# Front and passage of a transformer block with a spatial gMLP: a new order, and new engines for 44 operations

## The chip, the cores and the metric

The kernel runs on one core of a Trainium2 chip, in bf16 with f32 accumulation. The core has five engines with an instruction stream each, which wait for one another only through semaphores: PE (TensorE, matmuls), ACT (ScalarE), DVE (VectorE), POOL (GpSimd) and SP (SyncE, which here only issues DMAs). The metric is the device time of one execution, in microseconds.

## What is computed

With D = 448, S = 2048, 16 heads of 28, a window of 256 keys and F/2 = 896:

```python
mod = (silu(c) @ w_mod)                       # six rows of 448: sa, ca, ga, sb, cb, gb
h = layernorm(x) * (1 + ca) + sa
q, k, v = heads(h @ wqkv)
p = softmax(window(q @ k.T * 28 ** -0.5))     # key i seen by query t if 0 <= t - i < 256
x = x + ga * ((p @ v) @ wo)
h = layernorm(x) * (1 + cb) + sb
z = gelu(h @ w_in)
z1, z2 = z[:, :896], layernorm(z[:, 896:])
g = w_sp @ z2 + b_sp[:, None]                 # w_sp is 2048 x 2048, over the rows
out = x + gb * ((z1 * g) @ w_out)
```

## The kernel before

The 2048 rows are 16 tiles of 128, in four blocks (tb 0 to 3) of four tiles. Everything stays in the core's buffer (x_sb, hT, KT, Vaug and so on). The work falls into three stages, with overlaps.

The front and the attention. The modulation row is made by small matmuls (L546 and L536) of silu(c) with w_mod. wo_g is wo times ga (L601, four multiplies of 112 x 448, one for each quarter of the rows of wo); WQK is the q and k weight laid out in 32 columns a head (L617 on DVE and POOL, L618 on ACT). QBD, a buffer for a narrow piece of q, is cleared by two L523 on ACT. For each block: statistics of x (L629, L631 on DVE, the power on POOL in L633), the normalised tile xn (L644 to L657), a transpose to hT (matmuls at L740 for block 0, DMA at L465 for the rest), scale and shift (L732, L749, L751), the projections (K in L821, q in L763 and L797, v in L841), each copied out of the accumulator banks ps by ACT or DVE (L833/L834, L772, L802, L815/L816, L790/L791, L845/L846). For each tile: scores (L956 in blocks of 32 rows, L967 for the narrow piece), exponential on ACT (L912, into PW or PT), mask on DVE (L973, L993), times V (L1000), division by the row sum (L1014, L1016, into o_sb), DMA transpose (L465), the output projection (L1026) and the sum with x (L1030).

The passage. As the last tiles of the attention run, the second norm of each finished tile is made (again L629 to L657, into one of three xn slots), transposed by DMA into hT (L465), scaled and shifted when a block's four tiles are there (L1051 on DVE or POOL, L1049 on ACT; four pieces per block), and multiplied with w_in: L1120 for z2 and L1141 for z1, with gelu on ACT (L1127, L1149). DVE takes the statistics of z2 (L629) and normalises it (L1132). Meanwhile SP issues the transposing loads of w_sp into wspA and wspB (16 each, L465; L461 is the helper, `turn`). They write into buffers that the scores, the masks and QBD used, so each waits for the last reader. SP's loads and transposes are issued in one order on one queue.

The gated part. L1166 multiplies w_sp with all 16 tiles of z2, so its first sum needs the last z2 tile. Then come b_sp (L1170), z1 (L1173), w_out (L1185) and the store.

What sets the order: the program first adds 1148 operations, each with the engines that may do it (`either` and `free` offer ACT or DVE, or also POOL), its dependencies and the buffer slots it takes. The string PLAN (lines 13 to 73) then gives for each its engine (p, a, d, t for POOL, s for SP), its number and, behind dots, its slot. `Sched.order` reads the words, `count` and `waits` work out the semaphore waits, and `emit` issues each engine's operations in the order in which they stand:

```python
        for at, word in enumerate(PLAN.split()):
            n, *slots = map(int, word[1:].split("."))
            ...
            op.eng = names[word[0]]
            ...
            self.prog[op.eng].append(op)
```

Nothing is reordered later: an engine whose next instruction waits holds back all behind it.

Of the kernel before, what the change touches and what calls it, by code (L numbers as in the profile page):

```python
# [13 lines left out]
s10 t36 p40.1 a7 s8 p69.2 a9 p75.3 d114 s12 p65.1 p53.0 t33 d112 p68.2 s11 t34 p54.3 d115 p77.0 d113 p50.3 s13  # L14
a41 p71.0 t116 a43 p46.0 s15 d117.0 t29 p74.2 d118.3 p62.0 p64.2 p47 a42 a44 p57.0 p48.1 d106 d86 p76.0 p49
a107 t104 p129.6 p67.3 d87 d105 p126.4 t37 a130 p82.3 p56.3 t111 p84.1 d127 p81.1 p73.1 a131 p83.3 p66.0 d128
t38 p72.0 p141.1 d110 d121 p78.0 a108 t109 p70.2 p150.3 d119 p142 d122 d120 p79.2 d184 p151 t123 a143 p138.0
a152 t28 d125.2 p139 d124.3 p85.0 p147.6 d178 a140 p132.2 d185 p148 d182 a133 p144.7 d179 d180 p135.1 a134
p153.0 d183 a136 d181 p371.0 d246 t186 a137 p145 d248 p154 a372.4 t39 p165.1 d187.3 t190 d242 s194 p166 t188
a149 t192 d45 p377.0 a146 d373 p156.6 d167 a378.6 t189.1 p157 d244 p159.7 t191.2 a158 p395.0 d193.0 a155 s196  # L20
d379 p172.6 a396.5 d249 d247 p173 d243 p175.1 a174 s197 p160 d88 t89 d245 a397 p176 d168 p94.0 t250 p95 d177
s195 a171 p402.0 a161 d96 t254 p97.1 t256 a403.1 p98 d398 s14 d375 p162.7 d400 p374.0 p163 a404 d381 p90.0 d99
p376 d201 a199 p422.0 d198 d251.0 p380 p382 d200 p91 s258 a423.0.0 p211.1 d93 d92 d407 p218.0 d170 d252 p212
d255.1 t253.2 a164 d383 s260 p429.0 d169 a213 t257.3 p219 a430.3 p399.1 p205.1 s16 d220 p206 d384.2 p202.0
d306 s385 p203 a207 d426 p401 p447.0 a204 p208.1 s804 a448.4.1 d310 p209 d405 p227.0 d431 p228 s259 t102
p424.1 p406 p408 a425 p454.0 d229 a210 d409 p427.0 d312 a455.1 p230.0 t101 d410.1 p221.1 p231 d451 s411 t103
p428 p222 a232 p80.3 p472.0 d456 s261 a223 p432 a215 p224.0 d216 a473.5.2 p225 d214 s21 p233.1 p433 s807
p449.0 d434 t100 d226 a217 p479.0 d435.0 a450 t262 p234 d308 s436 a480.0 p474.0 p236.0 t263 d311 d313 d235
p452.0 p237 d476 s806 p453 a475 p496.0 a238 d307 d481 t265 d264 p412.1 a497.3.0 p457 p386.0 p387 p458 d309
d459 d388 d460.1 t314 t320 p413 p498.0 p521.0 a499 a522.1.1 p272.0 d414 p523.0 p273 p269.1 p477.0 s461 p270  # L30
d415 d274 d321.2 d316 s20 p503.0 a271 d500 t317.3 p275.0 p478 s323 p276 p266.1 p482 p267 a504.4 a524 p546.0
p483 t318 d389 d277 d319.1 a268 d505 d484 p282.0 d390 d278 p283 a547.5.2 p437.1 p548.0 p438 s18 d485.1 d525
p501.0 p528.0 d439 d440 d315.0 s486 s325 a284 a529.0 a549 a279 p502 p288.0 p291.1 p289 p292 d290 p553.0 d530
d293 p506 p507 p239.0 s322 p240 a554.3 a241 p526.1 t391 p527 s324 p531 a280 d550 p571.0 p532 p462.0 d508 d281
d416 d509.2 d392.1 d533 d441 t442 t417 a572.4.0 p463 p294.1 d534.1 d464 p295 p573.1 p578.0 a296 p300.0 s510
p285.1 p286 a579.0 p551.1 p301 p552 p595.0 d555 t329 t418 d327 d287 d302 d575 p511.1 p512 p556 d513 t328 a326
p557 a596.1.1 a574 p336.0 p337 p602.0 s535 p576.0 a338 p577 d558 d559.0 a603.3 p536.0 d393 p339.1 p537 p340
d580 p620.0 d538 d599 a341 p581 p297.0 p597.0 s17 p582 s394 p487.1 d465 p298 a621.6.2 d539 a598 a299 p488
p645.0 d583 p600.1 s808 d584.1 p622.1 p333.0 d489 p330.1 d624 d604 d466 p331 p334 a646.4.0 s585 d490 a332
p627.0 p601 t467 t443 t468 d335 d491 p346.1 d345 t444.1 p605 p347 p586.0 p587 a628.0 a348 p652.0 p358.1 d514  # L40
d649 a623 s560 a653.1 d588 p359 p606 p625.0 p349.0 p350 d629 a360 a351 p670.0 d589 d654 d607 p352.1 p303.0
p304 s19 a671.2.1 p353 p626 a344 a305 d608.2 t469.2 p630 p677.0 d354 d419.0 p631 p647.0 p364.1 p365 a678.6
p561.0 p562 d342 a648 p694.0 d420 t445 d674 d632 d343 d540 t470 s446 d633.0 p650.1 s803 a366 p672.1 d679 d563
a695.5.2 s609 d564 p367.1 p651 s421 t492 p655 p368 p656 p701.0 t541 a673 t542 d543.1 d657 p355.0 p675.0 a369
a702.3 t544 d658.2 p676 d493.0 p680 p356 d698 d565 d357 p681 p696.0 t566 d515 d682 p719.0 a697 d494 d590
a720.2.0 p699.1 d683.1 p700 s634 s471 p635.0 p636 p361.1 t516 t567 p726.0 d703 d637 p721.1 d638 p704 p705 p362
t779 s545 a727.4 s659 d723 d706 d568.1 p610.0 s495 a363 t778 p611 t517 s684 d707.2 d639 d728 d612 p744.0
t518.2 t777 t591 t569 p660.1 p724.1 p661 d662 a722 p725 s708 p729 a745.0.1 p730 p746.1 p751.0 p685.1 p686
p709.0 d731 d732.1 p710 a747 d748 d776 a752.1 p749.0 p750 p825.0 s570 d613 d753 p826.1 s733 d711 p754 p734.0
# [12 lines left out]
d904 p986.3 a1008 s809 t951 p987 d944 d834 t945 d888 p993.0 d898 a990 s811 d914 p994.1 a989 d920 d952 p995
# [1206 lines left out]
```

## Time and profile before

| | us |
|---|---|
| runs | 274.79, 276.12, 276.3 |
| median | 276.12 |
| profiled execution, its own time | 278.04 |
| its span, first to last instruction | 276.3 |
| TensorE busy | 268.3 (97%) |
| DVE, ACT, POOL busy | 162.9, 126.6, 110.1 |
| first L763 behind an L1030 on the chain | 47.27 |
| last block's L1120 begins | 141.12 |
| L1166 begins | 155.65 |

The span lies inside the execution's own time, which is 1.74 us longer. The granted TensorE clock is 1.0 throughout. Times in rows count from the span's start. Of a row of several instructions (x4) the length runs from the first one's start to the last one's end. A bracket behind a row gives the idle time ahead of it and what ended it.

### The profile page before, as it was taken

To read this page: it belongs to the slowest core of one execution; us is meant where nothing else is said; L and a number is where in the kernel's file an instruction comes from. 1 tells how busy PE (TensorE), PEld (TensorE's weight loads), DVE (VectorE), ACT (ScalarE), POOL (GpSimd) and SP (SyncE) were. 2 spreads that over 40 slices of the span, in tenths; PEclk is the share of its full clock that TensorE was granted. 3 is DMA by queue.
4 is the path that set the end of the run, shared out by engine and by line. 5 is a ranking of instruction groups with operands and counts; after the bars stand their busy time and mean duration, and the time that the engine had idled before them with its cause. 6 is when DMAs were issued, how large, how long until landed. Compare 5 with 4: busy or idle time off the path is not lost.

```text
span 276.3 us, 8381 instructions
## 1 busy us (share of the span) xinstructions
PE 268.3 (97%) x3751; PEld 153.2 (55%) x3751; DVE 162.9 (59%) x344; ACT 126.6 (46%) x149; POOL 110.1 (40%) x147
## 2 busy tenths in 40 slices
PE   8999999999999989999989999999999999999996
PEld 5976666677668756553534444444444444444453
DVE  3889999988899999948879401221313022152244
ACT  5899998898999979466755500000000000000000
POOL 6455188305042293546368003255353024062330
PEclk9999999999999999999999999999999999999999
DMA  7999767464333684969489997000000000001003
GB/s 213 311 230 137 100 138 93 121 100 108 63 108 78 63 80 64 156 149 136 105 163 191 203 187 130 0 0 0 2 0 0 0 2 0 33 17 36 33 33 116
DMA packets 67301, 25.54 MB, mean 92 GB/s; under 512 B 58497, under 2 KB 66178, under 8 KB 67266
## 3 DMA queue, kind: packets, MB, share of 16 engines
q1 hardware_dynamic: 66016, 24.02, 46.6%
q10 hardware_dynamic: 1250, 0.99, 1.3%
q8 instruction: 29, 0.48, 0.8%
q14 instruction: 6, 0.05, 0.1%
HBM read 9.01 MB, written 1.84 MB: 39 GB/s over the span
## 4 chain that ended last, share of the span: by engine, by line
PE 71%; DMA 9%; DVE 9%; ACT 4%; SPq 2%; POOL 2%; issue 1%; DVEq 0%
PE ps L1166 35%; PE ps L1185 8%; DMA wmodB<-in_w_mod_dram 5%; PE ps L1000 5%; PE ps L956 4%; DMA hT<-xn 4%; PE ps L1120 4%; PE ps L1026 3%; PE ps L1141 3%; DVE PT L973 3%; PE ps L763 3%; PE ps L821 3%; ACT PW L912 2%; PE ps L841 2%; DVE st_all L629 2%
## 5 line engine op out<-in xcount | busy, mean ns | idle before, releaser
L912 ACT ACTIVATE PW<-ps 128x2048 bf16<-128x2048 f32 (+1 forms) x42 | 59.9, 1450 | 6.4 <-PE ps L956 3.7
L1170 DVE TENSOR_TENSOR tmpg<-ps,bsp_bc 128x512 bf16<-128x512 f32 x28 | 18.9, 689 | 74.5 <-PE ps L1166 63.2
L1173 POOL TENSOR_TENSOR z1T<-tmpg,z1T 128x512 bf16<-128x512 bf16 x28 | 32.0, 1153 | 77.2 <-DVE tmpg L1170 77.2
L1166 PE MATMUL ps<-wspB,z 128*128 128x512 bf16 x224 | 50.1, 379 | 0.0
L1166 PE MATMUL ps<-wspA,z 128*128 128x512 bf16 x224 | 49.5, 379 | 0.0
L633 POOL TENSOR_TENSOR rs_all<-mv_all,neghalf 128x1 f32<-128x1 f32 (+2 forms) x37 | 23.4, 652 | 46.8 <-DVE mv_all L631 46.7
L1166 PEld LDWEIGHTS ps<-wspA,z 128*128 128x128 bf16 x224 | 21.8, 98 | 26.6 <-DVE z L1132 0.4
L1166 PEld LDWEIGHTS ps<-wspB,z 128*128 128x128 bf16 x224 | 21.9, 98 | 26.2
L973 DVE TENSOR_TENSOR PT<-PW,mask 128x2048 bf16<-128x2048 bf16 x28 | 35.3, 1266 | 0.0
L1000 PE MATMUL ps<-Vaug,PT 128*128 128x32 bf16 x496 | 26.0, 177 | 0.8 <-issue 0.6
L1000 PEld LDWEIGHTS ps<-Vaug,PT 128*128 128x128 bf16 x496 | 22.9, 96 | 4.1 <-issue 0.9
L1120 PE MATMUL ps<-w_in,hT 64*128 64x448 bf16 x224 | 22.0, 349 | 1.0 <-DVE st_all L629 1.0
L1141 PE MATMUL ps<-hT,w_in 64*128 64x512 bf16 x196 | 22.2, 376 | 0.2 <-ACT z L1127 0.2
L1185 PE MATMUL ps<-w_out_g,z1T 128*128 128x448 bf16 (+2 forms) x119 | 22.0, 341 | 0.0
L1000 PE MATMUL ps<-Vaug,PW 128*128 128x32 bf16 x224 | 21.3, 176 | 0.1
L629 DVE BATCH_NORM_STATS2 st_all<-x_sb 128x6 f32<-128x448 bf16 x32 | 19.2, 612 | 2.7 <-DMA x_sb<-in_A_x_dram 2.5
L629 DVE BATCH_NORM_STATS2 st_all<-z 128x6 f32<-128x448 bf16 x32 | 18.4, 607 | 3.2 <-ACT z L1127 3.1
L1000 PEld LDWEIGHTS ps<-Vaug,PW 128*128 128x128 bf16 x224 | 17.9, 96 | 2.1 <-issue 0.4
L956 PEld LDWEIGHTS ps<-qT,KT 32*128 32x128 bf16 (+1 forms) x1344 | 13.7, 90 | 9.7 <-ACT PW L912 6.2
L956 PE MATMUL ps<-qT,KT 32*128 32x128 bf16 (+5 forms) x1344 | 17.5, 197 | 1.5 <-issue 0.8
L1195 DVE TENSOR_TENSOR fin<-ps,x_sb 128x448 bf16<-128x448 f32 (+1 forms) x16 | 9.5, 612 | 16.1 <-PE ps L1185 11.6
L821 PE MATMUL ps<-hT,WQK 112*128 112x128 bf16 x256 | 18.4, 219 | 0.1
(108 smaller groups left out, 352.6 us busy)
## 6 DMA issues: line engine op xcount, KB each, us to landing
wmodB<-in_w_mod_dram SPq DMA_DIRECT2D x1, 1568.0 KB, 14.7
out_dram<-fin SPq DMA_DIRECT2D x14, 112.0 KB, 1.7
x_sb<-in_A_x_dram SPq DMA_DIRECT2D x3, 448.0 KB, 7.5
w_in<-in_B_w_in_dram SPq DMA_DIRECT2D x3, 448.0 KB, 4.4
w_out_g<-in_B_w_out_dram SPq DMA_DIRECT2D x1, 784.0 KB, 7.2
bsp_bc<-in_B_b_sp_dram SPq DMA_DIRECT2D x1, 512.0 KB, 5.4
x_sb<-in_A_x_dram SPq DMA_DIRECT2D x2, 224.0 KB, 4.6
hT<-xn SPq DMA_TRANSPOSE x28, 3.5
```

The costliest lines, as they stand in the source:

```text
L629: st = [dve(0.62, lambda e, t=t, o=12 - 6 * (n - ci), s=s: e.bn_stats(st_all[:, slot, t, o:o + 6], s()), deps(t), prio) for ci, s in enume ...
L633: return pool(0.4 + 0.15 * len(tiles), lambda e: e.tensor_tensor(rs_all[:, slot, a:b], mv_all[:, slot, a:b, 1], neghalf[:, 0:b - a], ALU.pow),
L821: km = lambda g, kc, start, stop, h=h, t=t: lambda e: e.matmul(ps[:, h.slot[0], g * 128:(g + 1) * 128], lhsT=WQK[0:CP, kc, 16 + 4 * g:20 + ...
L912: ex = act(xdur, lambda e, out_ap=out_ap, in_ap=in_ap: e.activation(out_ap(), in_ap(), ACT.Exp, scale=SCALE), [s] + list(after), v - 8.0 + ...
L956: fm.append(lambda e, hm=hm, qi=qi, key=key, kn=kn, lo=lo, hi=hi, col=col, p0=p0, t=t, j=j: e.matmul(ps[p0:p0 + kn, hm.slot[t], col:col + ...
L973: mk2 = lock_d(1.2, lambda e, hp=hp, at_w=at_w, pad=pad, at_f=at_f, cols=cols, j=j: e.tensor_tensor(cols(hp.slot[0] * 2048, [[256, 8], [12 ...
L1000: fns.append(lambda e, hp=hp, hO=hO, hi=hi, bi=bi, kb=kb, hd=hd, nb=nb, a=at[hi][bi], p_of=p_of: e.matmul(ps[:, hO.slot[0], 32 * hd:32 * h ...
L1120: return lambda e, kc, p0, start, stop: e.matmul(ps[:, hs[t % 2].slot[hf], 0:D], lhsT=hT[p0:p0 + 64, kc, t * 128:(t + 1) * 128], rhs=w_in[ ...
L1141: return lambda e, kc, p0, start, stop: e.matmul(ps[:, hs[b // 2].slot[b % 2], :], lhsT=w_in[p0:p0 + 64, kc, ft * 128:(ft + 1) * 128], rhs ...
L1166: m = pe(16 * MMS, [lambda e, h=h, si=si, ft=ft, tb=tb: e.matmul(ps[:, h.slot[0], :], lhsT=z2[:, si, ft * 128:(ft + 1) * 128], rhs=(wspA i ...
L1173: u = pool(1.16, lambda e, ht=ht, ft=ft, tb=tb: e.tensor_tensor(z1T[tb][:, ft, :], tmpg[:, ht.slot[0], :], z1T[tb][:, ft, :], ALU.mult), [ ...
L1185: return [lambda e, ft=ft: e.matmul(ps[:, h.slot[0], 0:hi - lo], lhsT=z1T[t // 4][:, ft, (t % 4) * 128:(t % 4 + 1) * 128], rhs=w_out_g[:, ...
```

## The change

Only PLAN changes: the same 1148 operations, with the same shapes, in another order and on other engines in two stretches, the front (to about 41 us) and the passage (about 108 to 158 us). The order in between, and all from L1166 on, is as before. 44 operations change engine, among them:

- POOL to DVE: two of the four L601 (wo_g), the copy of L583, two L617 (WQK), pieces of the second norm (L649, L651, L657) and three L1051.
- ACT to DVE: an L618, two L845, one L749, L730, L772, L790 and L815.
- DVE to ACT: two L617, one L751, L732, L846 and L1051, and two L816.
- DVE to POOL: three L656, one L649, L651 and L1051.

One line of the string, as an example of its form:

```diff
-s10 t36 p40.1 a7 s8 p69.2 a9 p75.3 d114 s12 p65.1 p53.0 t33 d112 p68.2 s11 t34 p54.3 d115 p77.0 d113 p50.3 s13
+s10 t36 p40.1 a7 s8 p69.2 a9 d114 p75.3 s12 p65.1 p64.2 d112 t33 p66.1 s11 p62.1 d115 d113 p71.3 p54.0 t116
```

What the words come to is seen in the engines' orders. First ScalarE at the start, from the loading of its exponential table (L521) to the first exponential (L912); L618 copies weights, L749 scales hT, L833 copies out K and L802 q. Before:

```order
L521 ACTIVATE ex_sb<-zero 128x2
L523 ACTIVATE QBD<-zero 128x1024
L618 ACTIVATE WQK<-wq_st 112x16x28
L749 ACTIVATE hT<-ps,modT 112x256 x2
L618 ACTIVATE WQK<-wq_st 112x16x28
L833 ACTIVATE KT<-ps 128x4x128 x2
L802 ACTIVATE qT<-ps 128x4x128
L749 ACTIVATE hT<-ps,modT 112x256 x4
L912 ACTIVATE PT<-ps 128x1024
```

And now:

```order
L521 ACTIVATE ex_sb<-zero 128x2
L618 ACTIVATE WQK<-wq_st 112x16x28
L749 ACTIVATE hT<-ps,modT 112x256 x3
L618 ACTIVATE WQK<-wq_st 112x16x28 x2
L523 ACTIVATE QBD<-zero 128x1024
L833 ACTIVATE KT<-ps 128x4x128 x2
L749 ACTIVATE hT<-ps,modT 112x256
L802 ACTIVATE qT<-ps 128x4x128
L749 ACTIVATE hT<-ps,modT 112x256 x2
L802 ACTIVATE qT<-ps 128x4x128
```

The second clearing of QBD (L523) has moved from the first place behind the table load to behind the weight copies, of which there is one more, and a second copy of q now stands ahead of the exponential.

Second, VectorE in the stretch in which wo_g is multiplied (in the trace of before from 33.49 to 41.2), between two reciprocals (L1014) of the attention. Before:

```order
L846 CAST Vaug<-ps 128x16x28
L1014 RECIPROCAL rec_all<-ps 128x16
L629 BN_STATS st_all<-x_sb 128x6
L1016 TENSOR_TENSOR o_sb<-ps,rec_all 128x4x112
L973 TENSOR_TENSOR PT<-PW,mask_60 128x2048 x2
L791 COPY QBD<-qT 32x512 x2
L1014 RECIPROCAL rec_all<-ps 128x16
```

And now:

```order
L846 CAST Vaug<-ps 128x16x28
L973 TENSOR_TENSOR PT<-PW,mask_60 128x2048
L1014 RECIPROCAL rec_all<-ps 128x16
L629 BN_STATS st_all<-x_sb 128x6
L1016 TENSOR_TENSOR o_sb<-ps,rec_all 128x4x112
L791 COPY QBD<-qT 32x512
L601 TENSOR_TENSOR wo_g<-wo_g,gg_sb 112x448
L973 TENSOR_TENSOR PT<-PW,mask_60 128x2048
L601 TENSOR_TENSOR wo_g<-wo_g,gg_sb 112x448
L791 COPY QBD<-qT 32x512 x2
```

Two of the four wo_g multiplies (L601) have come to VectorE from POOL, and one more narrow copy of q (L791, done on ScalarE as L790 before).

Third, SP's queue in the passage, from the load of w_out on; `hT<-xn` is a tile's second norm, `hT<-o_sb` the last tile's attention output. Before:

```order
L861 DMA w_out_g<-in_B_w_out_dram 128x7x448
L465 DMA_TRANSPOSE wspA<-in_B_w_sp_dram 128x1024 x2
L465 DMA_TRANSPOSE hT<-o_sb 128x4x128
L465 DMA_TRANSPOSE hT<-xn_91 128x4x128 x4
L465 DMA_TRANSPOSE wspB<-in_B_w_sp_dram 128x1024
L465 DMA_TRANSPOSE wspA<-in_B_w_sp_dram 128x1024 x2
L465 DMA_TRANSPOSE hT<-xn_91 128x4x128 x3
L465 DMA_TRANSPOSE wspA<-in_B_w_sp_dram 128x1024
L465 DMA_TRANSPOSE hT<-xn_91 128x4x128
L465 DMA_TRANSPOSE wspA<-in_B_w_sp_dram 128x1024 x5
```

And now:

```order
L861 DMA w_out_g<-in_B_w_out_dram 128x7x448
L465 DMA_TRANSPOSE wspB<-in_B_w_sp_dram 128x1024
L465 DMA_TRANSPOSE hT<-xn_91 128x4x128
L465 DMA_TRANSPOSE wspA<-in_B_w_sp_dram 128x1024 x2
L465 DMA_TRANSPOSE hT<-xn_91 128x4x128 x3
L465 DMA_TRANSPOSE hT<-o_sb 128x4x128
L465 DMA_TRANSPOSE wspA<-in_B_w_sp_dram 128x1024 x3
L465 DMA_TRANSPOSE hT<-xn_91 128x4x128
L465 DMA_TRANSPOSE wspB<-in_B_w_sp_dram 128x1024 x2
L465 DMA_TRANSPOSE hT<-xn_91 128x4x128 x3
```

In both lists the first four `hT<-xn` are the tiles of the third block, the next four those of the fourth. The fourth block's last one stands ten issues behind the third block's last, where it stood eight behind; the transpose of the last attention output has moved from ahead of them to between the blocks. The four pieces of scale and shift for the fourth block (L1051, L1049) were two on DVE and two on POOL, and are two on DVE, one on POOL and one on ACT.

118 lines of the change are left out of this document (59 added, 59 removed).

## Prediction

> **What bounds the kernel now.** I first read the busy line of the page, then TensorE's waits, then the chain of waits. The page:
>
> ```profile
> PE 268.3 (97%) x3751; PEld 153.2 (55%) x3751; DVE 162.9 (59%) x344; ACT 126.6 (46%) x149; POOL 110.1 (40%) x147
> ```
>
> TensorE is busy for 268.3 of 276.3 us, so an order can win only from its 8.0 idle us, much of it ahead of the first projection. Two rows of the waits of TensorE and its weight loads lie in the passage:
>
> ```profile
> PE ps L1120 <- DVE st_all L629: 1.0, 1, 1.0
> ...
> PEld ps L1166 <- DVE z L1132: 0.4, 1, 0.4
> ```
>
> The chain (start, length, what) shows what ends last at three places:
>
> ```profile
> 46.73 0.49 DVE x_sb L1030
> 47.27 0.61 PE ps L763 x2
> ...
> 141.12 5.46 PE ps L1120 x56
> 146.58 9.06 PE ps L1141 x84
> 155.65 76.08 PE ps L1166 x352
> ```
>
> Up to 46.73 the chain is on DVE, ACT and loads; from 47.27 mostly on TensorE. In the passage it goes through a transposing DMA, and from 141.12 it is TensorE alone. PE's order from shortly ahead of the row of 40.13 below up to its first L1120 is the same before and after, and so is all from L1166 on. So the change can act through **two numbers: when TensorE gets to L763 (47.27), and when L1166 starts (155.65)**.
>
> **The front.** Each row is start, length, engine, line. ScalarE:
>
> ```profile
> 7.25 1.04 ACT L523 ACTIVATE QBD<-zero 128x1024 f32<-128x1024 f32 x1
> ...
> 15.47 1.02 ACT L912 ACTIVATE PT<-ps 128x1024 bf16<-128x1024 f32 x1
> ...
> 25.43 1.88 ACT L912 ACTIVATE PW<-ps 128x2048 bf16<-128x2048 f32 x1
> ...
> 27.63 0.60 ACT L772 ACTIVATE qT<-ps 128x512 bf16<-128x512 f32 x1
> ...
> 37.54 0.63 ACT L790 ACTIVATE QBD<-qT 32x512 bf16<-32x512 bf16 x1
> 38.20 1.88 ACT L912 ACTIVATE PW<-ps 128x2048 bf16<-128x2048 f32 x1
> ```
>
> The second L523 (1.04) moves behind the weight copies and ahead of the K evacuations. It now delays those instead of filling a time when ScalarE was early; from the order the first L912 comes about 0.7 later. On TensorE both halves of the L536 columns come ahead of the first wide scores:
>
> ```profile
> 24.65 0.61 PE L956 MATMUL ps<-qT,KT 32*128 32x128 bf16 x48
> ...
> 25.41 0.53 PE L536 MATMUL ps<-sc_sb,wmodB 112*128 112x64 bf16 x12
> 25.77 0.29 PE L536 MATMUL ps<-sc_sb,wmodE 112*128 112x64 bf16 x4
> ...
> 40.13 0.61 PE L956 MATMUL ps<-qT,KT 32*128 32x128 bf16 x48 [0.34 <-ACT PW L912]
> ```
>
> The second half is 25.41 to 26.06, 0.65 long, so that the wide exponential of 25.43 comes at about 26.1: **+0.7**. ScalarE then gives it back: one L772 (0.60) and one L790 (0.63) leave it for DVE, 1.23 in all, before and just behind the exponential of 38.20. The first repays most of the 0.7, the second takes the rest and the 0.34 that PE waits at 40.13. By ScalarE alone, TensorE would be 0.5 to 0.9 early at 47.27.
>
> But there the chain names DVE. GpSimd's multiplies of wo_g (L601) and DVE's rows beside them:
>
> ```profile
> 34.91 6.06 POOL L601 TENSOR_TENSOR wo_g<-wo_g,gg_sb 112x448 bf16<-112x448 bf16 x4 [6.16 <-DMA wo_g<-in_A_wo_dram]
> ```
>
> ```profile
> 27.07 0.39 DVE L651 TENSOR_SCALAR xn<-x_sb,rs_all,nm_all 128x448 bf16<-128x448 bf16 x1
> ...
> 28.57 0.69 DVE L834 CAST KT<-ps 128x512 bf16<-128x512 f32 x1 [0.45 <-PE ps L821]
> ...
> 30.37 1.21 DVE L973 TENSOR_TENSOR PT<-PW,mask 128x2048 bf16<-128x2048 bf16 x1
> ...
> 35.19 3.82 DVE L973 TENSOR_TENSOR PT<-PW,mask 128x2048 bf16<-128x2048 bf16 x2
> 39.05 2.06 DVE L791 COPY QBD<-qT 32x512 bf16<-32x512 bf16 x2
> ```
>
> ```profile
> L791 DVE COPY QBD<-qT x7: 231/289/1021, 39.0 to 90.7; 32x512 bf16<-32x512 bf16 x7
> ```
>
> The last row gives minimum, median and maximum in ns. Alone, two L973 take 2.42 and two L791 0.58, so the four L601 cost DVE 3.82 − 2.42 + 2.06 − 0.58 = **2.9 us**. The Trainium skill, SBUF — State Buffer, section "Who interferes with whom", says that VectorE and GpSimd share one port pair by an exclusive lock and that whoever issues first holds it for a whole instruction; the trace agrees in kind, with 3.82 against 2.42.
>
> Now two of the four L601 run on DVE. L601 on DVE is not in the trace; its bounds are L791's 0.29 and L629's 0.61 (448 elements; a row further below), and I take 0.55, nearer to the row with 448 elements: 1.1 for two. DVE further takes L772 (0.7, as its L834, another copy out of the banks), one L651 (0.39) and the L790 (0.29, as L791): 2.5 in all. It saves half of the 2.9, 1.5. What remains, +1.0, is met by its earlier start there: at 28.57 DVE idled 0.45 for L821, and other pieces of the front leave it about 1.1 ahead. The bounds are a full relief (−1.5 more, one L601 held free of all contention) and none (+1.5). So DVE gets to L1030 0.1 to 1.2 early, ScalarE and TensorE 0.5 to 0.9: I take **−0.6**, with −1.5 and +0.3 as ends.
>
> **The passage.** The queue of SP issues all of these in turn:
>
> ```profile
> 118.68 5.19 SPq L465 DMA_TRANSPOSE hT<-xn  x4
> 123.92 2.24 SPq L465 DMA_TRANSPOSE wspB<-in_B_w_sp_dram  x1
> 126.20 2.64 SPq L465 DMA_TRANSPOSE wspA<-in_B_w_sp_dram  x2
> 128.88 4.83 SPq L465 DMA_TRANSPOSE hT<-xn  x3
> 133.75 1.30 SPq L465 DMA_TRANSPOSE wspA<-in_B_w_sp_dram  x1
> 135.11 1.25 SPq L465 DMA_TRANSPOSE hT<-xn  x1
> ```
>
> ```profile
> 118.68 2.39 DMA hT<-xn
> ...
> 122.61 4.17 DMA hT<-xn
> ...
> 135.11 4.16 DMA hT<-xn
> 139.30 0.41 DVE hT L1051
> 139.84 0.57 DVE hT L1051
> ```
>
> A transpose lands 2.39 to 4.17 after its issue, and an issue takes 1.25 to 1.32. The order puts the first tile of the third block earlier, but the last of that block keeps its place on the queue (issue done at 123.87), and TensorE did not wait there. The last tile of the fourth block was the 8th issue behind it; it is now the **10th**. Issued without a wait it starts at 123.87 + 9 × 1.3 = 135.6; before, the queue waited 0.94 (2.24 − 1.30) and 0.93 (4.83 − 3 × 1.3) over these rows. With one such wait half kept I take 136.2 (ends 135.6 and 137.5). With a landing of 3.3, the middle of 2.39 and 4.17, hT is there at 139.5, against 139.27.
>
> Then it is scaled (L1051). Before, two of the four pieces were GpSimd's and two DVE's:
>
> ```profile
> 139.37 1.69 POOL L1051 TENSOR_SCALAR hT<-hT,modT 128x512 bf16<-128x512 bf16 x2 [4.80 <-DMA hT<-xn]
> ```
>
> They ended at 141.06; PE's L1120 began at 141.12. So the wait that the view puts on DVE's st_all was GpSimd's: DVE's own last piece ended at 140.41. Now GpSimd has one piece, ScalarE one and DVE two, 1.14 in the rows above (139.30 to 140.41 with an L631 between), taken as 1.1. So TensorE can start at 139.5 + 1.1 = **140.6**, 0.5 earlier; its 14.53 of L1120 and L1141 bring it to L1166 at 155.1.
>
> L1166 also waits for the last normalised z (L1132) of DVE. In the stretch from 141.11 to 155.1 DVE had:
>
> ```profile
> L1132 DVE TENSOR_SCALAR z<-z,mv_all,rs_all 128x896 bf16<-128x896 bf16 x16 | 7.3, 505 | 0.0
> L629 DVE BATCH_NORM_STATS2 st_all<-z 128x6 f32<-128x448 bf16 x11 | 6.3, 608 | 0.9 <-ACT z L1127 0.9
> L631 DVE BATCH_NORM_AGGREGATE mv_all<-st_all 128x2 f32<-128x15 f32 x7 | 1.3, 201 | 0.0
> ```
>
> That is 14.9 busy with overlaps, in 14.0 − 0.9 = 13.1 us, a factor of 0.88. Behind its last L1051 DVE now has 15 L1132, 14 L629 and 9 L631: 15 × 0.456 + 14 × 0.573 + 9 × 0.186 = 16.5, times 0.88 = **14.5 us**, and no engine hides it. From 140.6 that ends at 155.1; with up to 0.5 of waits for z of L1127 (0.9 before), 155.6. I take L1166 at 155.4, **−0.2**. The ends: hT at 138.0 and TensorE limited by its own work (140.1, without the wait of 1.0, + 14.53 = 154.6), −1.0; the issue at 137.5 and the slow landing, +1.8 (below). These times stand on the clock of before; the front's gain comes on top, since xn and the buffers that the w_sp loads overwrite come free with the attention.
>
> **Sum.** −0.6 − 0.2 = −0.8. The profiled run takes 278.04 (span 276.3 and 1.74 around it) and would take 277.2; it lay 1.92 above the median of the three runs, 276.12, to which I apply the same difference: **275.3**. A measurement of this kernel tells about 0.5%, 1.4 us, from no change.
>
> **The rivals.**
>
> R1, both parts give their full value, **273.5**. GpSimd's remaining two L601 fall on rows of DVE that cost little, so that of the 2.9 nearly all goes, DVE reaches L1030 1.5 early and ScalarE's 1.23 comes through (−1.5); the last transpose lands in 2.39 and TensorE starts on its work alone (−1.0). For it: 0.34 at 40.13, the waits of 1.0 and 0.4. Against it: TensorE has little idle time, and DVE's 14.5 behind hT.
>
> R2, the other side: **the last transpose of the second norm stuck behind w_sp loads on SP's queue, 277.7**. Five w_sp loads now stand between the two blocks' last transposes, against four, and the transpose of the last attention output is there as well. If both waits of before (0.94 and 0.93) recur, it is issued at 137.5 and with 4.17 lands at 141.7; DVE's two pieces and 14.5 us of backlog, now queued behind that landing, end at 157.3: +1.7. With a front of −0.6 to +0.3 that is 277.2 to 278.1. It decides when the landing comes later than 140.1; before, DVE had some of that backlog ahead of the wait, and was through by the end of the stretch above, 155.1.
>
> R3, contention stays though two L601 moved, **277.0**: each L601 left on GpSimd holds a DVE instruction for its length (4 L601 in 6.06, 1.5 each, 3.0 for two, as much as the 2.9 of four), so DVE's 2.5 of new work has nothing against it but its lead of 1.1: +1.4 at DVE, less 0.5 that its idle time absorbs, so the front gives +0.9 and the passage nothing. By the lock rule of the Trainium skill, SBUF — State Buffer, section "Who interferes with whom", this is the case in which GpSimd issues first at each of the two; half the cost for half the instructions is what the rows 3.82 and 2.06 suggest.
>
> That the change moves nothing is excluded by the order, in which 44 operations have another engine.
>
> **How the numbers follow.** The forecast, within 0.5%: 0.42. R1: 0.30, all faster. R2: 0.21, slower. R3: 0.07, within 0.5%. So faster 0.30, same 0.49, slower 0.21. R1's lower half and R2's upper half are left out: 273.2 to 278.0.
>
> **What would show it.** The front: the first wide exponential near 26.1 instead of 25.43, the L973 and L791 beside L601 together near 4.5 instead of 5.88, and TensorE at its first L763 behind L1030 at 46.7 instead of 47.27. The passage: SP's last hT transpose issued at 136.2 (−0.6), the wait of L1120 shorter, L1166 starting 0.8 earlier than 155.65. I am wrong if L973 beside L601 stays as long as before, if that transpose lands later than 140.1, or if TensorE shows a wait on a line that it did not wait for.

## The result and the profile after

Over 15 runs each, the changed kernel took a median of **278.16 us** (276.32 to 279.10) and the kernel before 276.12 us (274.61 to 277.59): a ratio of **1.007**, 95% interval 1.0047 to 1.0094. It is slower by 0.7%, where 0.3% faster was forecast, and lies 0.16 us outside the range. Three later comparisons, of 12 runs each, gave 1.0043 (1.0011 to 1.0075), 1.0050 (1.0015 to 1.0085) and 1.0057 (1.0027 to 1.0087); the kernel before against itself gave 1.0009, 1.0045 and 1.0002, so that a single ratio is good to some 0.4%. Pooled over these four comparisons, without the few runs that lie over 1.5% above their kernel's fastest, 48 runs of the changed kernel have a median of 278.08 and 140 of the kernel before 276.57: 1.5 us. By the words of the two PLANs it is 45 operations that change engine, one more than was said above.

The profiled execution after took 278.13 us, with a span of 276.4. The busy line, to be held against 268.3, 162.9, 126.6 and 110.1:

```profile
PE 269.0 (97%) x3751; PEld 153.1 (55%) x3751; DVE 164.1 (59%) x352; ACT 127.2 (46%) x150; POOL 100.9 (37%) x138
```

GpSimd lost 9 us of work, VectorE and ScalarE gained 1.2 and 0.6, and TensorE is as full as before. Its waits:

```profile
PE ps L821 <- DVE hT L732: 0.8, 1, 0.8
PE ps L821 <- ACT hT L749: 0.6, 1, 0.6
PE ps L1000 <- issue: 0.5, 2, 0.3
PE ps L546 <- DMA wmodA<-in_w_mod_dram: 0.5, 1, 0.5
PE ps L956 <- issue: 0.4, 2, 0.2
```

The wait of L1120 for st_all (1.0), which was forecast to be shorter, is gone. In its place stand waits in the front: L821 for L749 near 10 us and for L732 near 28 us. The chain behind the front:

```profile
48.67 0.54 PE ps L763 x2
...
141.41 4.73 PE ps L1120 x50
...
155.77 76.08 PE ps L1166 x352
```

L763 is 1.4 later than before (47.27), L1120 0.3 later, L1166 0.1 later. Held against the one profile of before, the front thus lost 1.3 us (TensorE at L956, in the table below) and the passage won 1.1 (from the first L1120 to L1166), and the two profiled executions (278.04 and 278.13) are alike. But 278.13 is the changed kernel's median, while 278.04 is 1.92 above that of before. The question is what the profiled execution of before had that the others have not.

Where the prediction named rows, VectorE in the profile after reads (start, length, engine, line):

```profile
37.99 0.85 DVE L791 COPY QBD<-qT 32x512 bf16<-32x512 bf16 x1
38.87 0.63 DVE L601 TENSOR_TENSOR wo_g<-wo_g,gg_sb 112x448 bf16<-112x448 bf16 x1
39.41 1.22 DVE L973 TENSOR_TENSOR PT<-PW,mask 128x2048 bf16<-128x2048 bf16 x1
40.54 0.62 DVE L601 TENSOR_TENSOR wo_g<-wo_g,gg_sb 112x448 bf16<-112x448 bf16 x1
41.19 1.45 DVE L791 COPY QBD<-qT 32x512 bf16<-32x512 bf16 x2
```

And GpSimd at the same time:

```profile
36.41 2.28 POOL L601 TENSOR_TENSOR wo_g<-wo_g,gg_sb 112x448 bf16<-112x448 bf16 x2 [8.41 <-DMA wo_g<-in_A_wo_dram]
40.14 3.14 POOL L732 TENSOR_SCALAR hT<-hT,modT 112x512 bf16<-112x512 bf16 x3 [1.45 <-DMA hT<-xn]
```

L601 on VectorE takes 0.62 (0.55 was taken). L973 is back at 1.22, but L791 is not: two take 1.45, alone 0.58. GpSimd, done early with L601, goes on to L732 (three in 3.14) while VectorE is at L791. The contention moved to another partner.

### The profile page after: what moved, and what is told of

The parts are those of the page before. It is cut to its first block, busy times and chain, and to the rows that moved or that the text cites. A ratio compares the mean times of both kernels' runs of the same rounds, so it can differ in the third digit from the quotient of the medians.

```text
span 276.4 us, 8384 instructions
## 1 busy us (share of the span) xinstructions
PE 269.0 (97%) x3751; PEld 153.1 (55%) x3751; DVE 164.1 (59%) x352; ACT 127.2 (46%) x150; POOL 100.9 (37%) x138
## 4 chain that ended last, share of the span: by engine, by line
PE 80%; ACT 5%; DVE 5%; DMA 3%; POOL 2%; SPq 1%; issue 1%; ACTq 1%; POOLq 0%; DVEq 0%
PE ps L1166 35%; PE ps L1120 8%; PE ps L1141 8%; PE ps L1185 8%; PE ps L1000 5%; PE ps L956 4%; ACT PW L912 4%; PE ps L1026 4%; PE ps L763 3%; PE ps L821 3%; DMA wq_st<-in_A_wqkv_dram 3%; PE ps L841 2%; DVE st_all L629 1%; POOL xn L651 1%; SPq L465 1%
## 5 line engine op out<-in xcount | busy, mean ns | idle before, releaser
L912 ACT ACTIVATE PW<-ps 128x2048 bf16<-128x2048 f32 (+1 forms) x42 | 59.9, 1449 | 7.3 <-PE ps L956 4.2
L1166 PE MATMUL ps<-wspB,z 128*128 128x512 bf16 x224 | 50.1, 379 | 0.0
L1166 PE MATMUL ps<-wspA,z 128*128 128x512 bf16 x224 | 49.5, 379 | 0.0
L1166 PEld LDWEIGHTS ps<-wspA,z 128*128 128x128 bf16 x224 | 21.9, 98 | 26.6 <-issue 0.4
L1166 PEld LDWEIGHTS ps<-wspB,z 128*128 128x128 bf16 x224 | 21.9, 98 | 26.2
L973 DVE TENSOR_TENSOR PT<-PW,mask 128x2048 bf16<-128x2048 bf16 x28 | 33.8, 1214 | 0.2 <-ACT PW L912 0.2
L1000 PE MATMUL ps<-Vaug,PT 128*128 128x32 bf16 x496 | 26.0, 177 | 0.7 <-issue 0.5
L1000 PEld LDWEIGHTS ps<-Vaug,PT 128*128 128x128 bf16 x496 | 22.8, 96 | 4.6 <-DVE PT L973 0.4
L1141 PE MATMUL ps<-hT,w_in 64*128 64x512 bf16 x196 | 23.0, 376 | 0.0
L1120 PE MATMUL ps<-w_in,hT 64*128 64x448 bf16 x224 | 22.8, 349 | 0.0
L1000 PE MATMUL ps<-Vaug,PW 128*128 128x32 bf16 x224 | 21.2, 176 | 0.0
L821 PE MATMUL ps<-hT,WQK 112*128 112x128 bf16 x256 | 18.0, 219 | 1.6 <-DVE hT L732 0.8
L956 PEld LDWEIGHTS ps<-qT,KT 32*128 32x128 bf16 (+1 forms) x1344 | 13.6, 90 | 9.8 <-ACT PW L912 7.1
L1127 ACT ACTIVATE z<-ps 128x896 bf16<-128x896 f32 x16 | 14.2, 914 | 10.2 <-PE ps L1120 10.2
L1000 PEld LDWEIGHTS ps<-Vaug,PW 128*128 128x128 bf16 x224 | 17.9, 96 | 1.7
```

The source lines that it names most:

```text
L821: km = lambda g, kc, start, stop, h=h, t=t: lambda e: e.matmul(ps[:, h.slot[0], g * 128:(g + 1) * 128], lhsT=WQK[0:CP, kc, 16 + 4 * g:20 + ...
L912: ex = act(xdur, lambda e, out_ap=out_ap, in_ap=in_ap: e.activation(out_ap(), in_ap(), ACT.Exp, scale=SCALE), [s] + list(after), v - 8.0 + ...
L956: fm.append(lambda e, hm=hm, qi=qi, key=key, kn=kn, lo=lo, hi=hi, col=col, p0=p0, t=t, j=j: e.matmul(ps[p0:p0 + kn, hm.slot[t], col:col + ...
L973: mk2 = lock_d(1.2, lambda e, hp=hp, at_w=at_w, pad=pad, at_f=at_f, cols=cols, j=j: e.tensor_tensor(cols(hp.slot[0] * 2048, [[256, 8], [12 ...
L1000: fns.append(lambda e, hp=hp, hO=hO, hi=hi, bi=bi, kb=kb, hd=hd, nb=nb, a=at[hi][bi], p_of=p_of: e.matmul(ps[:, hO.slot[0], 32 * hd:32 * h ...
L1120: return lambda e, kc, p0, start, stop: e.matmul(ps[:, hs[t % 2].slot[hf], 0:D], lhsT=hT[p0:p0 + 64, kc, t * 128:(t + 1) * 128], rhs=w_in[ ...
```

## The experiments

Each kernel differs from one of the two only in PLAN. "Parts" are joined at word p571 (61.5 us in the profile of before), where both plans have the same order on every engine: the words of one plan up to there, then those of the other that are not among them. The kernels marked e2, e3 have line numbers one lower. Theories A (front costs, passage gains, profile of before not typical), B (front neutral), C (the prediction) and, later, D to G are told in the expectations.

All profiles are read with the same rule: the starts of five TensorE groups, the first L821, the wide L956 that started at 52.61 in the profile before, the first L1120, the L1120 that started at 131.62 there, and the first L1166. Columns are the start of the first and the times from each to the next; the last is the idle time of TensorE between 8 and 152 us that the trace puts down to nothing but "issue". L1166 is taken at its first weight load: 13 of the 18 traces have 438 records of L1166 matmuls instead of 448, the first one is among those missing, and in them rows and waits of L1166 show its start 0.23 late.

| kernel (front, passage) | L821 starts | to L956 | to L1120 | to 2nd L1120 | to L1166 | L1120 to L1166 | issue |
|---|---|---|---|---|---|---|---|
| before, shown (old, old) | 9.36 | 43.25 | 56.46 | 22.55 | 23.96 | 46.51 | 1.58 |
| e1 before (old, old) | 9.35 | 42.75 | 55.52 | 22.20 | 22.77 | 44.97 | 0.41 |
| e12 before (old, old) | 9.37 | 43.14 | 55.16 | 22.20 | 22.77 | 44.97 | 0.68 |
| e16 before (old, old) | 11.83 | 43.27 | 56.24 | 22.20 | 22.77 | 44.97 | 1.38 |
| e2 (new, old) | 9.55 | 43.02 | 57.16 | 22.20 | 22.77 | 44.97 | 2.79 |
| e9 (new, old) | 9.74 | 42.86 | 56.92 | 22.20 | 22.77 | 44.97 | 1.39 |
| e3 (old, new) | 9.74 | 43.04 | 55.87 | 22.72 | 22.77 | 45.49 | 0.75 |
| e10 (old, new) | 9.46 | 43.02 | 55.22 | 22.42 | 23.54 | 45.96 | 0.44 |
| after, first (new, new) | 10.90 | 43.04 | 56.37 | 22.61 | 22.77 | 45.39 | 0.95 |
| e4 after (new, new) | 9.28 | 43.09 | 55.76 | 22.61 | 22.77 | 45.39 | 0.89 |
| e11 after (new, new) | 10.80 | 43.29 | 55.97 | 22.42 | 23.17 | 45.60 | 0.73 |
| e15 after (new, new) | 9.49 | 42.91 | 56.26 | 22.84 | 22.77 | 45.61 | 1.00 |
| e5 (new, changed; new) | 10.47 | 43.28 | 56.52 | 22.61 | 23.29 | 45.90 | 1.55 |
| e6 (new, changed; new) | 9.98 | 43.50 | 57.03 | 23.06 | 22.77 | 45.84 | 1.95 |
| e7 (new; mixed) | 9.46 | 42.69 | 56.54 | 24.65 | 22.78 | 47.44 | 1.26 |
| e8 (old; mixed) | 9.89 | 43.68 | 56.19 | 24.50 | 22.78 | 47.28 | 1.20 |
| e13 (old to 10 us, then new; new) | 9.37 | 44.21 | 57.75 | 22.42 | 22.77 | 45.19 | 2.35 |
| e14 (new to 10 us, then old; old) | 9.72 | 43.12 | 55.74 | 22.20 | 22.77 | 44.97 | 0.70 |

**e1, the kernel before again.** No edit.

> The kernel before, unchanged, for a second profile. Theory A (the front costs, the passage gains, and the profiled execution shown of before was a slow one of its kind): ratio 1.000 within 0.003, and a span of about 274.4 us, 1.9 less than 276.3, with the difference in waits that come and go (landings of loads up to the first L821, 9.36 us, and instruction fetch, 2.1 us in five stalls of TensorE). Theory B (the front is neutral and what is seen there is the landing of wq_st, 9.27 us after against 8.2): the second profile shows L821 starting as late as 10.9 us in some execution of before as well.

Measured: ratio 1.0009 (0.9980 to 1.0039), span 273.3, 3.0 less than in the profile shown. The waits of TensorE:

```profile
PE ps L565 <- DVE st_all L489: 1.1, 1, 1.1
PE ps L821 <- ACT hT L749: 0.4, 1, 0.4
PE ps L956 <- ACT PW L912: 0.3, 1, 0.3
PE ps L956 <- issue: 0.2, 1, 0.2
PE ps L967 <- ACT PW L912: 0.2, 1, 0.2
PE ps L1166 <- issue: 0.2, 1, 0.2
```

This is the same program as in the prediction's rows, without the wait of L1120 that the prediction meant to remove, and with 0.41 of "issue" instead of 1.58. (The 0.2 at L1166 is the missing record and not a wait.) The first L821 starts at 9.35 in both, so B's landing of the loads is not what parts them. Of theory A, the half on the profile of before holds.

**e2 and e9, the new front with the old passage; e3 and e10, the old front with the new passage.**

```diff
 e2, e9:  PLAN = words of after up to p571  + the other words as in before
 e3, e10: PLAN = words of before up to p571 + the other words as in after
```

> The new order up to about 60 us, the old one behind it, the passage among it. Theory A: slower than before by 1.3 to 2.5 us (the shift of +1.25 us that TensorE has at its first L1120 in the profile after, and up to 1.1 more where the old passage keeps its wait), TensorE at the first L821 at 10.5 to 11 us, and a wait of L821 for L732 near 27 us. Theory B: within 0.8 us of before. Theory C (the prediction's front): 0.6 us faster.

> The old order up to about 60 us, the new passage. Theory A: faster than before by 0.5 to 1.1 us, and no wait of TensorE of 1.0 us at the last block's L1120. Theory B: slower by 1.3 to 2.5 us. Theory C (the prediction's passage): 0.2 us faster.

> The new front with the old passage, a second time: second profile, and twelve more times. Theory A (front and passage cost about as much each, and the costs add): 0.4 to 1.1 us slower than before. Theory F (the new front costs through the loads: their landing has a late form, the fourth wmodA at 7.6 us instead of 6.7 and the last x_sb at 16.3 instead of 14, seen in three of six profiles with the new front and in none of four with the old one): the late form in about half of the profiles of this front and of none of the old. Theory G (the late form is chance of an execution): it shows in old fronts as well. Fetch: TensorE's stall for instructions in the L1000 near 53 us (0.10 to 0.39 us in six of six profiles of the new front, none in four of the old) shows again.

> The old front with the new passage, a second time. Theory A: 0.3 to 0.9 us slower than before: 22.6 to 22.7 us from the first L1120 to the fourth block's first L1120 against 22.2, less the wait of 1.0 us where an execution of before has it. Rival (the passage is neutral and the front has it all): within 0.2. Theory F: loads in their early form. Fetch: no stall near 53 us.

Measured: e2 1.0016 (0.9990 to 1.0042), e9 1.0010 (0.9973 to 1.0048); e3 1.0010 (0.9984 to 1.0037), e10 1.0032 (1.0000 to 1.0063). The times cannot tell either part from no change. The profiles can. The passage of the kernel before, in e12 (start, length; the last block's L1120 and L1166 are the last two rows):

```profile
107.67 1.69 PE L1120 MATMUL ps<-w_in,hT 64*128 64x448 bf16 x16
...
114.55 3.19 PE L1141 MATMUL ps<-hT,w_in 64*128 64x512 bf16 x28
117.57 5.46 PE L1120 MATMUL ps<-w_in,hT 64*128 64x448 bf16 x56
122.86 5.56 PE L1141 MATMUL ps<-hT,w_in 64*128 64x512 bf16 x50
128.35 0.93 PE L1026 MATMUL ps<-wo_g,hT 112*128 112x448 bf16 x4
129.22 0.82 PE L1141 MATMUL ps<-hT,w_in 64*128 64x512 bf16 x6
129.88 5.46 PE L1120 MATMUL ps<-w_in,hT 64*128 64x448 bf16 x56
...
138.19 5.46 PE L1120 MATMUL ps<-w_in,hT 64*128 64x448 bf16 x56
...
152.88 5.34 PE L1166 MATMUL ps<-wspA,z 128*128 128x512 bf16 x24 [0.16 <-issue]
```

And the new passage, in e10:

```profile
107.70 1.69 PE L1120 MATMUL ps<-w_in,hT 64*128 64x448 bf16 x16
...
113.44 1.03 PE L1141 MATMUL ps<-hT,w_in 64*128 64x512 bf16 x8
114.31 0.73 PE L1120 MATMUL ps<-w_in,hT 64*128 64x448 bf16 x6
114.87 1.03 PE L1141 MATMUL ps<-hT,w_in 64*128 64x512 bf16 x8
...
127.09 0.55 PE L1026 MATMUL ps<-wo_g,hT 112*128 112x448 bf16 x2
127.58 0.82 PE L1141 MATMUL ps<-hT,w_in 64*128 64x512 bf16 x6
128.33 0.55 PE L1026 MATMUL ps<-wo_g,hT 112*128 112x448 bf16 x2
128.81 1.47 PE L1141 MATMUL ps<-hT,w_in 64*128 64x512 bf16 x12
130.12 4.89 PE L1120 MATMUL ps<-w_in,hT 64*128 64x448 bf16 x50
...
139.09 4.91 PE L1120 MATMUL ps<-w_in,hT 64*128 64x448 bf16 x50 [0.49 <-DVE hT L1051]
...
153.89 4.48 PE L1166 MATMUL ps<-wspA,z 128*128 128x512 bf16 x20 [0.26 <-DVE z L1132]
```

From the start at 107.67 and 107.70, the first weight load of L1166 comes 44.97 and 45.96 later. The new order takes L1120 and L1141 in turns of 6 and 8. These turns cost nothing. The matmuls of both lines start in pairs. From the starts of the rows above, a pair of L1141 takes 0.216 (28 matmuls in 3.02) and a pair of L1120 0.189 (56 in 5.29) in the long runs of the old order, and the same in the short turns of the new one (8 in 0.87, 6 in 0.56). Also, from the 2nd L1120 of the table to L1166, a stretch with seven changes in the new order and three in the old, both take 22.77 where nothing waits. What costs is the last tile's output projection, L1026: its four matmuls, of another shape, stood in one break of L1141 and now stand in two breaks of two. Each break costs 0.10 ahead of its first L1026 and 0.10 behind its last: four L1026 take 0.87 to the next L1141 in one break and 0.49 + 0.48 in two, and the six L1141 between take 0.75 instead of 0.65. Where nothing waits, the second break makes most of the difference of 22.42 against 22.20 (e10, e11, e13), and short waits for hT L1051 bring it to 22.61 to 23.06. In the table the old passage takes 44.97 in **six of seven** profiles and 46.51 in the one that was shown; the new one takes 45.19 to 45.96, a mean of 45.60 over nine. So the passage does not gain: it costs 0.63 against the usual old passage and 0.41 against the mean of seven. A's gain of the passage and C's are refuted; A's "the two cost about as much each" stays possible by the times.

The front: from the first L821 to the L956 the seven old fronts take 43.16 in the mean (42.75 to 43.68), the nine whole new ones 43.08 (42.69 to 43.50). It is neutral. A's cost of 1.3 there is refuted, and so is C's gain of 0.6; B holds for this stretch.

**e4, e11 and e15, the changed kernel again; e12 and e16, the kernel before.** No edit.

> The changed kernel, unchanged, for a second profile on the same chip as the three others. All theories: 1.3 to 2.6 us slower than before. Theory A: the first L821 starts at 10.5 us or later and L821 waits for L732 near 27 us again. Theory B: those two places differ from profile to profile by as much as between before and after.

> The changed kernel, a third profile and more times: 1.2 to 2.0 us slower than before. Theory A: as much as the front alone and the passage alone together. Theory F: the late form of the loads with a chance of one half. Fetch: the stall near 53 us again.

> The kernel before, a third profile and more times: ratio 1.000 within 0.003. Theory F: loads in their early form; theory G: the late form possible. The wait of 1.0 us at the last block's L1120, seen in one of three profiles of the old passage, shows with a chance of one third. Fetch: no stall near 53 us.

> The changed kernel, a fourth profile. Theory F: the late form with a chance of one half (four of eight profiles with the new first 10 us so far). Theory G: as e16.

> The kernel before, a fourth profile. Theory F: early form. Theory G: the late form with the same chance as in the changed kernel. The ratio to itself shows how far this measurement can be trusted: two earlier ones gave 1.0009 and 1.0045.

The ratios stand in the section on the result. The loads have a late form: in the first profile after, e5, e6 and e11 the first L821 starts at 9.98 to 10.90. e16 shows it in the kernel before, worse:

```profile
PE ps L546 <- DMA wmodA<-in_w_mod_dram: 2.2, 2, 2.0
```

So the late form comes with the old front too, is worth up to 2.5 us, and is not a mark of the new front alone, as F had it. Whether it is more frequent there (four of nine profiles against one of seven) is not shown; the mean start is 9.86 for seven old fronts and 9.96 for nine new. The stretch between L956 and the first L1120, in which both kernels have the **same order on all engines** up to GpSimd's first difference at 103 us, does differ: 55.81 in the mean of the seven with the old front (55.16 to 56.46), 56.50 of the nine with the new (55.76 to 57.16). The new passage has no part in it: behind the old front e3, e10 and e8 take 55.22 to 56.19. Of these 0.69, TensorE's "issue" makes 0.52 (0.69 against 1.21 in the means, within this stretch). One such stop is tied to the new front:

```profile
53.62 0.22 PE L1000 MATMUL ps<-Vaug,PT 128*128 128x32 bf16 x2 [0.32 <-issue]
```

This row is e15's. The same matmul stops for 0.10 to 0.39 in all nine profiles with the whole new front, and in none of the nine others. The trace has the packet of instructions that precedes it (16 KB, the page's queue "q8 instruction") start at 51.0 to 52.9 in these nine, at 48.8 to 50.4 in six of the seven with the old front, and at 51.4 in e16, whose whole front runs 2.5 late.

**e13 and e14, the first 10 us exchanged.**

```diff
 e13: PLAN = words of before up to p142 + the other words as in after
 e14: PLAN = words of after up to p142  + the other words as in before
```

> The old order up to TensorE's second group of L821 (about 10 us), the changed kernel behind it; SP's and ACT's loads stand in the same order in all kernels. Theory F (something in the new order of the first 10 us brings on the late form of the loads): the early form (last of the four wmodA by 7.2, last x_sb by 15.1), the first L821 at 9.3 to 9.9 us, and at 52 us at most 52.8. Theory G (chance of an execution): the late form (last x_sb at 16.1 or later) possible here too; then the first L821 at 10 us or later. Fetch: the stall near 53 us as in the changed kernel. Time: by F 0.5 to 1 us faster than the changed kernel, by G the same.

> The new order of the first 10 us, the kernel before behind it. Theory F: the late form of the loads with a chance of one half, and then the first L821 at 10 us or later and 53.5 us or more where the kernel before has 52.1 to 52.6. Theory G: as likely as in the kernel before (none in three profiles of it, none in six with the old first 10 us). Fetch: no stall near 53 us.

Measured: e13 1.0048 (1.0022 to 1.0074), e14 1.0014 (0.9984 to 1.0044). Loads in their early form in both, so they do not decide between F and G by themselves; e16 refutes F as it was put. The L1000 near 53 us does not stop in e13, though all behind 10 us is new there. That was not expected: in these profiles the stop needs the whole new front. e13 paid at another place, 0.8 for L740 waiting for xn L644, since old and new orders do not fit together there. From L956 to the first L1120 e13 takes 57.75 and e14 55.74: in these two single profiles the long stretch goes with the new order behind 10 us, and not with that of the first 10 us.

**e5, GpSimd's L651 no longer beside VectorE's L732.**

```diff
-d93 d256 d254 d92 d200 d251.0 d199 d198 d99
+d93 d92 d200 d251.0 d199 d198 d256 d254 d99
```

> The changed kernel, but DVE's two L649 that feed GpSimd's two L651 (second block's third x) stand behind the three L732 of block 1, so that GpSimd's L651 no longer runs beside them. Theory A (the new collision costs: in the changed kernel L732 x2 took 1.47 us beside 1.82 us of L651, against 0.74 in the kernel before, and L821 then waited 0.65 to 0.79): L732 x2 at 0.75 to 0.85, the wait of L821 at 0 to 0.1, TensorE 0.6 to 0.8 earlier at the wide scores near 28, and what is left of it at 52 us (the L956 that started at 52.37 in the last profile of the changed kernel, 52.10 in that of before) is 0.3 to 0.7. Theory D (DVE bounds the front near 41 us anyway): the wait goes, but at 52 us nothing is left, within 0.1. The whole: 0 to 0.7 us faster than the changed kernel, too little for the timing.

Measured: 1.0045 (1.0018 to 1.0072). GpSimd's L651 in e4, the changed kernel:

```profile
24.59 1.82 POOL L651 TENSOR_SCALAR xn<-x_sb,rs_all,nm_all 128x448 bf16<-128x448 bf16 x2 [1.24 <-DMA hT<-xn]
```

VectorE's L732 beside it:

```profile
25.09 1.47 DVE L732 TENSOR_SCALAR hT<-hT,modT 112x512 bf16<-112x512 bf16 x2
```

GpSimd's L651 in e5, 3.5 later:

```profile
28.12 1.58 POOL L651 TENSOR_SCALAR xn<-x_sb,rs_all,nm_all 128x448 bf16<-128x448 bf16 x2 [3.17 <-DVE nm_all L649]
```

VectorE's L732 in e5, now done before it:

```profile
26.54 0.41 DVE L732 TENSOR_SCALAR hT<-hT,modT 112x512 bf16<-112x512 bf16 x1 [0.89 <-DMA hT<-xn]
27.17 0.73 DVE L732 TENSOR_SCALAR hT<-hT,modT 112x512 bf16<-112x512 bf16 x2
```

The collision is real (1.47 against 0.73) and this edit takes it away. But the wait of L821 stayed at 0.4, because in this execution the transposes of hT landed late (0.89), and from the first L821 to the L956 it took 43.28, no less than the changed kernel's 42.91 to 43.29. A's 0.3 to 0.7 are a miss. That fits theory D, that something later in the front bounds it, but with the late transposes this one profile does not show it.

**e6, all four L601 on GpSimd again.**

```diff
-d101 ... d102 ... t103 t100
+t102 t101 t103 t100
```

> The changed kernel with all four L601 on GpSimd again, as before. Theory A (the move paid less than forecast, because GpSimd, done earlier, ran its L732 beside DVE's L791): GpSimd's L601 x4 take 6.0 us, DVE's L973 and L791 beside them 5.4 to 5.9 as before, and TensorE at 52 us is within 0.4 of the changed kernel, either way. Forecast of the record (the move is worth 0.4 net: 1.1 of new work against 1.5 of contention): 0.4 later at 52 us. Theory D: 0.5 earlier, since DVE loses 1.24 us of work.

Measured: 1.0072 (1.0043 to 1.0101). GpSimd in e6, with the four L601 in one row:

```profile
36.05 5.20 POOL L601 TENSOR_TENSOR wo_g<-wo_g,gg_sb 112x448 bf16<-112x448 bf16 x4 [8.51 <-DMA wo_g<-in_A_wo_dram]
```

VectorE beside them:

```profile
37.52 0.84 DVE L791 COPY QBD<-qT 32x512 bf16<-32x512 bf16 x1
38.40 1.95 DVE L973 TENSOR_TENSOR PT<-PW,mask 128x2048 bf16<-128x2048 bf16 x1
40.38 1.80 DVE L791 COPY QBD<-qT 32x512 bf16<-32x512 bf16 x2
```

These rows of VectorE take 4.59; with two L601 among them, the five rows after take 0.85 + 0.63 + 1.22 + 0.62 + 1.45 = 4.77. For VectorE the move is worth nothing: the five rows take 4.29 to 4.84 in the eight new fronts that have it. A's 6.0 for GpSimd and 5.4 to 5.9 for VectorE are missed, and D's 0.5 earlier did not come. To the L956 e6 took 43.50, 0.4 more than the mean of the changed kernel's four (43.08), the size that the record gave for the move; in one profile it is at the edge of the scatter.

**e7 and e8, TensorE's old order in the new passage.**

```diff
-p827 p828 p841.3 p842.2 p953.0 p843 p954.1 p844 p955 p857.3 p956 p858.2
+p827 p828 p841.3 p842.2 p843 p844 p953.0 p954.1 p955 p956 p857.3 p858.2
```

> The changed kernel with TensorE's old order in the passage (L1120 and L1141 in two runs each instead of five between 108 and 131 us); the other engines keep the new order. Theory A (each change between L1120 and L1141 costs TensorE some 0.1 us): from the first L1120 to the L1120 of the fourth block's first pair 22.2 us instead of 22.6, no new wait, 0.4 us faster than the changed kernel. Theory E (the new order was needed by the new order of loads): a wait of TensorE of 0.3 us or more appears at an L1120 or L1141 of the third block, and nothing is won.

> The old front, and in the passage the new order of SP, DVE, ACT and POOL with TensorE's old order. Theory A: 22.2 us over the stretch named above, no wait of 1 us at the last block's L1120, 0.4 us faster than the new passage with the old front; against the kernel before 0 to 0.6 us faster, the size of the wait that comes in some of its executions. Theory E: a wait of 0.3 us or more in the third block, no faster than before.

Measured: e7 1.0118 (1.0091 to 1.0145), e8 1.0129 (1.0108 to 1.0149), 6 runs each. In e7 TensorE's waits are:

```profile
PE ps L1120 <- ACT z1T L1149: 1.2, 1, 1.2
...
PE ps L1026 <- DVE x_sb L1030: 0.9, 1, 0.9
```

The stretch takes 24.65 and 24.50. Theory E holds, with other waits than it named: the new order of the loads, of ScalarE and VectorE needs TensorE's new order. Theory A was wrong about the turns, which cost nothing (above). By the starts of TensorE's matmuls the two stops take 2.4 in e7 and 2.3 in e8, which leaves 22.2. So the 0.2 belong to TensorE's new order, but this exchange does not win them back.

## Why the prediction was wrong

Three terms failed. The front was to give −0.6 and gave −0.1, the passage was to give −0.2 and cost 0.4, and the stretch between them, which was put at nothing, cost 0.7.

1. **The passage** (−0.2, from TensorE 0.5 earlier at the last L1120). This step failed on its base: the wait of 1.0 at L1120 came in one of seven profiles of the old passage, the one shown. There the last transpose of the second norm landed 4.16 after its issue; in the six others it took 2.49 to 2.69, and this L1120 did not wait. The mechanism was right. In the first profile after, GpSimd has one L1051 instead of two, and no wait is left:

```profile
137.90 0.77 POOL L1051 TENSOR_SCALAR hT<-hT,modT 128x512 bf16<-128x512 bf16 x1 [1.77 <-DMA hT<-xn]
```

When that transpose lands late, the new order even wins about what was forecast: the last block's L1120 starts 1.83 behind the landing in the profile of before and 1.28 behind it in e10 and e5, which also land late (4.59 and 4.68 behind the issue); the forecast had 1.1. R2 needed a landing 31.0 behind the first L1120 (140.1 − 109.07); in the new passage it comes at most 30.11 behind it, so R2 did not happen. But usually nothing was there to win, and the step left out what TensorE's own new order costs: 0.2, most of it from the second break by L1026, and waits for hT L1051 in the third block of up to 0.6. With it the passage costs 0.41 in the mean.

2. **The front** (−0.6). Measured −0.1 in the mean, with a scatter of 0.3. ScalarE was late by less than was forecast: counted from the first L821, the first wide exponential starts at 16.37 in the mean of the nine new fronts against 16.09 of the seven old, 0.3 later instead of 0.7. The 0.34 at L956 was won: that wait for L912 stands in all seven old fronts (0.34 to 0.38) and in none of the nine new. What failed is VectorE's account, and TensorE shows it at a line where it did not wait before: near 27 us L821 waits 0.39 to 0.88 for VectorE's L732 in all nine new fronts and in none of the seven old. VectorE's L973 and L791 beside L601 were to fall from 5.88 to about 4.5. In the profile after they take 0.85 + 1.22 + 1.45 = 3.52 for one L973 and three L791, which alone take 0.29 + 1.22 + 0.58 = 2.09: 1.4 of contention is left of 2.9, the half that was taken. But e1, the same program as before, had less to lose:

```profile
35.17 4.08 DVE L973 TENSOR_TENSOR PT<-PW,mask 128x2048 bf16<-128x2048 bf16 x2
39.28 1.33 DVE L791 COPY QBD<-qT 32x512 bf16<-32x512 bf16 x2
```

That is 5.41 against 3.00 alone, 2.4; from there the relief is 1.0. The seven old fronts take 5.12 to 5.88 here, and the profile shown took the most. The two L601 cost 1.25 on VectorE, not 1.1. The lead at L834 that was to meet this was 1.1 in the forecast. L834 in e1 (start, length):

```profile
28.55 0.69 DVE L834 CAST KT<-ps 128x512 bf16<-128x512 f32 x1 [0.45 <-PE ps L821]
```

The same instruction in e4:

```profile
27.98 0.68 DVE L834 CAST KT<-ps 128x512 bf16<-128x512 f32 x1
```

It is 0.6 earlier. And L651 beside L732 is a new collision, 1.47 against 0.73, for which the working had no term. So relief 1.0 and lead 0.6 stand against 2.6 of new work (the 2.5 of the forecast with L601 at 0.62): 1.0 late by this account. Measured, again from the first L821 and by the means, VectorE starts its first L1030 at 37.00 in the new fronts against 36.79 in the old, 0.2 late instead of 0.1 to 1.2 early; and TensorE is at its L763 at 37.74 against 37.84, 0.1 early instead of 0.6. How far ScalarE's relief of 1.23 made up for VectorE is not told apart here, nor how much of the wait at L821 the collision alone makes: in e5, without it, late transposes left a wait of 0.39. The Trainium skill, SBUF — State Buffer, section "Who interferes with whom", names copy, cast and tensor_scalar among the operations that can hold the shared port pair; the trace agrees with 1.47 against 0.73 for L732, and with 1.45 against 0.58 for L791. Rival R3, contention that stays, was near in kind, but its price of +0.9 was not paid.

3. **What was not in the sum at all**: the stretch between, with the same order in both up to 103 us. It takes 0.69 longer behind the new front, 0.52 of it stops of TensorE for instructions (see the last section). The sum had no term for it. The prediction took it as unchanged because the order is.

4. **The base.** "It lay 1.92 above the median" stood in the prediction, and the same difference was carried over. What set that execution apart was in good part the wait that the change was to remove: e1, which took 275.03, lacks that 1.0 and has 0.41 of issue instead of 1.58. A change can't take away from the median what the median doesn't have.

Put together by means: start +0.1, front −0.1, stretch between +0.69, passage +0.41: +1.1 us, against 1.5 from the pooled medians. Open are the rest, and how far each is from chance: with seven and nine profiles and a scatter of 0.5 in the stretch between, its 0.69 is uncertain by about as much as 0.5, and the two parts timed alone (0.1 and 0.2%) add up to less than the 0.55% of the whole, though with intervals of some 0.3% each this too can be chance. Why TensorE stops longer for instructions behind the new front, and at the L1000 near 53 us in every profile, is not known.

## What to carry to other kernels

A wait in one profile is a property of that execution until a second profile shows it; when the profiled run is far above the median, look for the difference first in the waits that the change is to remove. On an engine that is 97% busy, price its own new order (here one more break of paired matmuls by matmuls of another shape, 0.2 us) before the waits of others. And work taken from an engine frees it to start its next work earlier: see what that then runs beside.

## What the runs showed of the hardware

The trace puts some of TensorE's stops down to nothing but "issue". Those of more than 0.06 us come, but for two of 0.07, at ten fixed places in its order (near 35, 53, 62, 72, 76, 85, 90, 94, 98 and 101 us). Two things tie them to the fetching of instructions. Next to one another, these places lie 127 or 128 matmuls apart, or two or four times that, which with one weight load for each matmul is about 256 instructions or a multiple. And each of the 53 stops of 0.2 us or more, over 18 profiles, ends 1.22 to 1.56 us behind the end of a 16 KB packet of the queue "q8 instruction" of the page, of which one comes about every four us in this stretch. A stop lasts up to 0.86 us; an execution has two to seven of more than 0.06 us, and they sum to 0.41 to 2.79. That is a part of the spread of this kernel, 274.3 to 279.7; late loads are another. The Trainium skill, Runtime: NRT & Kernel Launch, section "Instruction fetch mechanics", has blocks of 16 KiB fetched by DMA while the engine runs, at a cost "mostly hidden"; the 29 packets of 0.48 MB agree with the blocks, and most of them bring no stop, but the cost is not always hidden here.

The first loads can land late in an execution: TensorE's first L821 starts at 9.98 to 11.83 in five of the 18 profiles and at 9.28 to 9.89 in the others. The last transpose of the second norm lands 2.42 to 2.69 after its issue in most profiles, and 3.92 to 4.68 in five.
